# A transformer kernel on one core: two blocks side by side at the start of the dense mixture, weight conversions moved out of attention, another beginning

## The chip, the cores and the metric

One core of a Trainium2 chip. The metric is device time in microseconds of one execution of the whole program. Engines: TensorE (matmuls), VectorE (DVE), ScalarE (ACT), GpSimd (POOL), SyncE (SP, which issues most DMAs).

## What is computed

Three parts in a row, all in float32 with float64 inputs where the inputs came as such (the two weight matrices `w_in` and `w_out` of the first mixture arrive as float64 and are converted on the chip from their two 32-bit words).

```python
# 1. attention: batch 4, 8 heads, 512 local and 32 global positions, head size 64
s_g = scale * q_g @ concat(k_g, k_l).T;  out_g = softmax(s_g) @ concat(v_g, v_l)
s_ll = where(|i - j| <= 32, scale * q_l @ k_l.T, -1e9);  s_lg = scale * q_l @ k_g.T
out_l = softmax(concat(s_lg, s_ll)) @ concat(v_g, v_l)
x = concat(out_g, out_l) as 2176 tokens of 512
# 2. first mixture (dense): w_in 512 x 2048, w_out 2048 x 512
h = x @ w_in
g = where(h >= 1, h, where(h <= -1, 0, (h + 1) ** 2 / 4))
y = g @ w_out
# 3. second mixture: 8 experts, one chosen for each token
logits = (y / |y|) @ (emb / |emb|).T / tau;  e = argmax;  gate = softmax(logits)[e]
out = gate * (relu(y @ w1[e]) @ w2[e])
```

## The kernel before, in words

**Attention** runs in eight units (`Unit`, L310): unit n is batch n // 2 and four of the eight heads. A unit has four quarters k = 0 to 3. A quarter is: `scores` (L427: 16 small matmuls, then on VectorE a mask with a running minimum, on ACT an exponential), `fin` (L475: reciprocals on VectorE, normalising on GpSimd), `trans` (L491: transposes on TensorE, copies on ACT), `pval` (L512: the product with the values, copied to SBUF by ACT) and, after every second one, `gsum` (L538: a sum on VectorE and the store of the result to DRAM). Once per unit come `glob_s`, `glob_n` and `glob_t` (L383 to L425): the global queries' scores, their normalising on GpSimd, their transposes. Keys and queries of a unit are loaded by `ld_qk`, put in pair order by `pair` (a copy, on ACT for k and on VectorE for q, but on VectorE for unit 0), transposed and spread by `tr_k` and `tr_q`. `glob_load` and `glob_tr` (L161, L167) load and transpose the global keys and queries of all four batches, once.

**The order** is one list: `events` (L553) gives each step a mark, 16 marks to a unit and four to a quarter, and each engine's queue, SP's too, gets its instructions in the order of the marks. The offsets are in the table `AT` (L22): quarter k of unit n has its scores at 16 n + 4 k, its transposes 9.34 later, its value product 13.59 later. Each engine works strictly in its own order.

**Conversions.** `conv_load` (L232) loads a raw tile of 512 KB (128 rows of 512 float64); `conv_half` (L248) converts half of one: three bit operations on VectorE (L214, L217, L220); for a half of `w_in` then a rounded copy `winh` on ACT (L257) and the rest `winl` on GpSimd (L258). There are 32 raw tiles, 64 halves. `seq` (L228) is their order: 12 tiles of `w_in`, 12 of `w_out`, 4 of `w_in`, 4 of `w_out`. The marks `CV` and counts `CN` (L28) put 40 halves in attention; the other 24 go into the slots of the mixture's block 0. Two buffers hold raw tiles; the load of tile n + 2 is issued when tile n is converted.

**First mixture.** 17 tiles of 128 tokens in six blocks of 3, 3, 2, 3, 3 and 3 tiles. A slot g is one block bi and one f of 16: `up1` (L709: 12 matmuls, x and w_in each split into a rounded part and a rest, into a PSUM buffer `hps`, of which there are two), `act1` (L723: ReLU, square, then on VectorE the minimum and maximum, and by `wout` L743 the split of one row block of w_out), `act1b` (L739: the rest on VectorE), and, two slots later (LAG), `down1` (L751: 9 matmuls into `yp`). The main loop (L1322) walks g, block after block. A block's x comes back from DRAM by `x_load` (L681) and is split by `x_split` (L691) during the block before. When a block is done `y_out` (L608) copies and stores its output tiles, and the router's work on them (`logits`, 8 dot products on VectorE a tile, `choose`, `route3`) is spread by `pieces` (L776) over the slots of the next block; 3, 2, 3, 3, 3 and 3 tiles after the six blocks. `embed_bc` (L622) loads eight broadcast rows of 256 KB for them. Two up projections, `up1(0)` and `up1(1)`, are issued at the end of attention (marks 185.66 and 202.01), after all of its steps.

**Second mixture.** The most frequent expert runs densely over all blocks, the other tokens in gathered quads. The change does not touch it.

Of the kernel before, what the change touches and what calls it, by code (L numbers as in the profile page):

```python
# [9 lines left out]
F32 = mybir.dt.float32  # L10
# [22 lines left out]
def kernel(  # L33
# [19 lines left out]
    P = 128  # L53
# [107 lines left out]
    def glob_load(src, tag, bufs):  # L161
        t = mx.tile([P, H, D], F32, name="gl", tag=tag, bufs=bufs)
        for b in range(B):
            nc.sync.dma_start(out=t[b * G : (b + 1) * G], in_=src[b].rearrange("h s d -> s h d"))
        return t

    def glob_tr(src, isq):  # L167
        pt = ps.tile([P, NP, P], F32, name="pgl", tag="T")
        for hp in range(NP):
            nc.tensor.transpose(pt[:, hp, :], src[:, 2 * hp : 2 * hp + 2, :].rearrange("p h d -> p (h d)"), ident)  # L170
        if isq:
            nc.vector.tensor_copy(out=qgz[0:D, :, 0, :], in_=pt[0:D])
            nc.vector.tensor_copy(out=qgz[D:P, :, 1, :], in_=pt[D:P])
        else:
            nc.vector.tensor_copy(out=kgT, in_=pt)
# [49 lines left out]
    nin, nout = KD * DFF // CL, KF * DM // CL  # L225
    craw = {}

    seq = [*range(3 * KD), *range(nin, nin + 12), *range(3 * KD, nin), *range(nin + 12, nin + nout)]  # L228
    NCV = len(seq)
    ncv = sum(CN) // 2  # L230

    def conv_load(n):  # L232
        if n >= NCV:
            return
        i = seq[n]
        if i < nin:
            f, k = divmod(i, KD)
            src = win_u[:, k, 2 * f * CL : 2 * (f + 1) * CL]
        else:
            src = wout_u[:, i - nin, :]  # L240
        if n < ncv + 2:
# [4 lines left out]
        nc.sync.dma_start(out=raw.rearrange("p n t -> p (n t)"), in_=src)  # L246

    def conv_half(n, h):  # L248
        c0 = h * CC
        i = seq[n]  # L250
        raw = craw[n][:, c0 : c0 + CC, :]
        if i < nin:
            f, k = divmod(i, KD)
            wf = mx.tile([P, DM], F32, name="wf", tag="wf")[:, :CC]
            conv(raw, wf)
            hi = winh[2 * f + h][:, k, :]
            nc.scalar.copy(out=hi, in_=wf)  # L257
            nc.gpsimd.tensor_tensor(out=winl[2 * f + h][:, k, :], in0=wf, in1=hi.bitcast(F32), op=ALU.subtract)  # L258
        else:
            conv(raw, wof[(i - nin) // 2][:, (i - nin) % 2, c0 : c0 + CC])  # L260
# [1166 lines left out]
```

## Time and profile before

| | us |
|---|---|
| median of 3 runs (794.5 to 796.12) | 794.64 |
| the profiled execution's own time | 794.92 |
| its span, first to last instruction | 793.1 |
| TensorE busy | 759.5 |
| VectorE busy | 504.2 |
| ScalarE busy | 404.2 |
| GpSimd busy | 145.6 |

The profiled execution is one run; its span leaves out what lies before the first and after the last instruction. Busy times are sums over the span. A busy TensorE is not one at its peak: its instructions are pipelined and their ends are modelled. The program's stages follow each other: attention to about 166 us, the first mixture to about 558, then the second. The chain of waits is followed back from the last instruction: at each step to what released it.

### The profile page before, as it was taken

The page shows a single profiled execution, that of the slowest core. Times are in us where ns is not written, and L with a number is a line of the kernel's source. Part 1 is how long each engine was busy: PE and PEld are TensorE (multiplying, and loading weights), DVE is VectorE, ACT ScalarE, POOL GpSimd, SP SyncE. Part 2 cuts the span into 40 slices and gives each one's busy share as a digit, 9 for nine tenths or more (in the row PEclk, how much of TensorE's full clock was granted, in tenths as well). Part 3 has the DMA queues.
Part 4 walks back from the last instruction along what each step waited for, and adds up shares of the span by engine and source line. Part 5 has one row for each costly group of instructions (what it writes and reads, how often), then busy time and mean ns, then how long its engine had stood idle before and what let it go on. Part 6 is the DMA issues. An engine that isn't in the chain of part 4 may idle for free.

```text
span 793.1 us, 14812 instructions
## 1 busy us (share of the span) xinstructions
PE 759.5 (96%) x5115; PEld 640.8 (81%) x5115; DVE 504.2 (64%) x1513; ACT 404.2 (51%) x1011; POOL 145.6 (18%) x301
## 2 busy tenths in 40 slices
PE   6989986999999999999999999999999999999997
PEld 4767765789899898999889988989888777778775
DVE  3889986969876678867676677888786211221111
ACT  2989986845655556764655565665311121112100
POOL 4778885612100000000000001000002101010001
PEclk7899998989999999999999999999999999999999
DMA  7777877653252002001002001223207389454321
GB/s 184 202 211 225 221 195 216 189 160 121 81 160 66 2 1 80 1 28 40 0 1 67 1 1 67 93 79 90 73 0 265 100 308 309 136 179 120 107 93 37
DMA packets 73072, 89.40 MB, mean 113 GB/s; under 512 B 27440, under 2 KB 47920, under 8 KB 72992
## 3 DMA queue, kind: packets, MB, share of 16 engines
q1 hardware_dynamic: 71312, 83.42, 34.9%
q0 software_dynamic: 1680, 4.98, 1.6%
q8 instruction: 42, 0.69, 0.4%
q14 instruction: 38, 0.31, 0.1%
HBM read 79.77 MB, written 13.65 MB: 118 GB/s over the span
## 4 chain that ended last, share of the span: by engine, by line
PE 56%; issue 20%; DVE 11%; DMA 6%; ACT 4%; POOL 3%; SPq 1%; POOLq 0%; ACTq 0%; DVEq 0%
PE hps L718 22%; PE yp L761 22%; DMA out<-ob,ide 4%; PE eh L1186 2%; PE eo L1208 2%; DVE wf L217 1%; DVE sm L451 1%; ACT sm L461 1%; PE pv L524 1%; DVE wf L220 1%; POOL out L1220 1%; PE s L439 1%; PE ta L501 1%; PE pv L535 1%; DMA raw<-in_moe_w_out 1%
## 5 line engine op out<-in xcount | busy, mean ns | idle before, releaser
L718 PE MATMUL hps<-xh,winh 128*128 128x384 f32 (+1 forms) x384 | 126.3, 329 | 0.0
L718 PE MATMUL hps<-xl,winh 128*128 128x384 f32 (+1 forms) x384 | 126.1, 328 | 0.0
L718 PE MATMUL hps<-xh,winl 128*128 128x384 f32 (+1 forms) x384 | 125.7, 327 | 0.0
L761 PE MATMUL yp<-wol,gh 128*128 128x512 f32 x272 | 107.5, 395 | 0.0
L761 PE MATMUL yp<-woh,gh 128*128 128x512 f32 x272 | 107.3, 395 | 0.0
L1192 DVE SCALAR_TENSOR_TENSOR el<-eh,eg 128x384 fp32r<-128x384 f32 (+1 forms) x48 | 25.7, 535 | 118.4 <-ACT eg L1191 110.4
L1191 ACT ACTIVATE eg<-eh 128x384 fp32r<-128x384 f32 (+1 forms) x48 | 22.7, 474 | 120.5 <-PE eh L1186 108.7
L718 PEld LDWEIGHTS hps<-xh,winh 128*128 128x128 f32 x384 | 72.6, 189 | 4.0
L718 PEld LDWEIGHTS hps<-xh,winl 128*128 128x128 f32 x384 | 72.5, 189 | 3.8
L718 PEld LDWEIGHTS hps<-xl,winh 128*128 128x128 f32 x384 | 72.4, 189 | 0.0
L748 DVE TENSOR_TENSOR wol<-wof,woh 128x512 fp32r<-128x512 f32 x96 | 66.4, 692 | 1.3
L1186 PE MATMUL eh<-exh,wh 128*128 128x384 f32 (+1 forms) x192 | 65.3, 340 | 0.0
L1186 PE MATMUL eh<-exl,wh 128*128 128x384 f32 (+1 forms) x192 | 62.8, 327 | 0.0
L1186 PE MATMUL eh<-exh,wl 128*128 128x384 f32 (+1 forms) x192 | 62.7, 326 | 0.0
L1220 POOL DMA_INDIRECT out<-ob,ide x17 | 17.3, 1019 | 230.1 <-DVE ob L1217 227.0
L747 ACT CAST woh<-wof 128x512 fp32r<-128x512 f32 x96 | 58.0, 605 | 0.1
L461 ACT ACTIVATE sm<-sm,st 128x160 f32<-128x160 f32 x128 | 53.4, 426 | 8.5 <-DVE st L451 8.5
L761 PEld LDWEIGHTS yp<-wol,gh 128*128 128x128 f32 x272 | 51.1, 188 | 8.0
L761 PEld LDWEIGHTS yp<-woh,gh 128*128 128x128 f32 x272 | 51.1, 188 | 7.9
L483 POOL TENSOR_SCALAR pn<-sm,st 128x128 f32<-128x128 f32 x128 | 53.7, 438 | 19.0 <-DVE st L479 11.2
L1208 PE MATMUL eo<-wl,eg 128*128 128x512 f32 x136 | 53.8, 395 | 0.1
L1208 PE MATMUL eo<-wh,el 128*128 128x512 f32 x136 | 53.6, 394 | 0.0
(904 smaller groups left out, 1664.0 us busy)
## 6 DMA issues: line engine op xcount, KB each, us to landing
rw<-in_moe_w SPq DMA_DIRECT2D x128, 256.0 KB
raw<-in_moe_w_in SPq DMA_DIRECT2D x16, 512.0 KB
raw<-in_moe_w_out SPq DMA_DIRECT2D x16, 512.0 KB
k<-in_k_l SPq DMA_DIRECT2D x16, 256.0 KB
q<-in_q_l SPq DMA_DIRECT2D x16, 256.0 KB
xsc<-xs SPq DMA_DIRECT2D x16, 256.0 KB
ysc<-y SPq DMA_DIRECT2D x16, 256.0 KB
rw<-in_moe_w SPq DMA_DIRECT2D x8, 512.0 KB
```

The costliest lines, as they stand in the source:

```text
L217: nc.vector.scalar_tensor_tensor(out=du, in0=hi, scalar=0xC0000000, in1=du, op0=ALU.bitwise_and, op1=ALU.bitwise_or)
L461: nc.scalar.activation(out=sm[:, i, :], in_=sm[:, i, :], func=AF.Exp, scale=-1.0, bias=st[:, 0, i : i + 1], accum_out=st[:, 1, i : i + 1],)
L483: eng_of[AT["f4"][i]].tensor_scalar(out=pn[:, i, :].rearrange("p (c x) -> p c x", c=2), in0=sel(sm[:, i, :]), scalar1=st[:, 2, i : i + 1], ...
L718: nc.tensor.matmul(hp_[:, :n], lhsT=wt[:, kk, fs], rhs=xt, start=kk == 0 and i == 0, stop=kk == KD - 1 and i == 2)
L747: nc.scalar.copy(out=woh, in_=wof[f // 2][:, f % 2, :])
L748: nc.vector.tensor_tensor(out=wol, in0=wof[f // 2][:, f % 2, :], in1=woh.bitcast(F32), op=ALU.subtract)
L761: nc.tensor.matmul(B_.yp[i], lhsT=gt[:, cs], rhs=wt, start=f == 0 and k == 0, stop=f == KF - 1 and k == 2)
L1186: nc.tensor.matmul(hps[:, :n], lhsT=w[:, fs], rhs=x, start=kk == 0 and i == 0, stop=kk == KD - 1 and i == 2)
L1191: nc.scalar.activation(out=gh, in_=hps[:, :n], func=AF.Relu)
L1192: nc.vector.scalar_tensor_tensor(out=gl, in0=hps[:, :n], scalar=0.0, in1=gh.bitcast(F32), op0=ALU.max, op1=ALU.subtract)
L1208: nc.tensor.matmul(B_.yp[i], lhsT=a[:, cs], rhs=w, start=f == 0 and k == 0, stop=f == KF2 - 1 and k == 2)
L1220: nc.gpsimd.indirect_dma_start(out=outs[t], out_offset=bass.IndirectOffsetOnAxis(ap=ide[:, t : t + 1], axis=0), in_=ob, in_offset=None, bo ...
```

## The change

Five things. (1) Blocks 0 and 1 of the first mixture alternate, f by f (`items`), so that one split of `w_out` serves both (`wout`); block 1's sums take the PSUM buffers of tag T; x of both blocks is loaded and split in attention, x of block 2 at the end of the pair. (2) 18 halves are converted in attention, at other marks (`CV`, `cmarks`), and 46 in the pair's slots, in order of need: for each eighth m of the inner dimension two tiles of `w_in` and two of `w_out`. A tile of `w_in` now holds two row blocks of 256 columns. (3) The beginning: the first q load is issued on ACT's queue, only batch 0 of the global keys and queries is loaded and transposed before unit 0's global scores, the rest in units 0 and 1; the second quarter's scores of unit 0 move from mark 4 to mark 1; raw loads start later; 26 more small matmuls (`warm`). (4) The copies of k to pair order go to VectorE; the two early up projections move from behind all steps of attention to marks 134.5 and 136.5, ahead of the last value product (137.59). (5) `pieces` is computed by a rule and takes 0, 3, 4, 4, 3 and 3 tiles after the six blocks; output tiles 3, 4, 5 and 10 get other buffers (`YOB`).

```diff
-    ld_v=13.82, k0=10.74, q0=11.3, k1=15.74, q1=14.98, xl=116.97, xs=129.29, u0=185.66, u1=202.01, rk0=6.13,
-    rq0=8.31, rk1=11.03, rq1=11.75, e_k='A', e_q='V', e_g='P', bp=1, ev=10, le='PVPVV', e_kc='A', e_kd='A',
+    ld_v=13.82, k0=10.74, q0=11.3, k1=15.74, q1=14.98, xl=70.0, xs=84.9, xl1=118.5, xs1=130.1, u0=134.5, u1=136.5, rk0=6.13,
+    rq0=8.31, rk1=11.03, rq1=11.75, e_k='V', e_q='V', e_g='P', bp=1, ev=10, le='PVPVV', e_kc='A', e_kd='A',
...
-CV = [8.84, 10.77, 11.32, 11.44, 13.36, 16.6, 17.6, 23.12]
-CN = [4, 6, 4, 4, 4, 6, 6, 6]
+CV = [1.2, 5.2, 8.8, 12.84]
...
-    seq = [*range(3 * KD), *range(nin, nin + 12), *range(3 * KD, nin), *range(nin + 12, nin + nout)]
-    NCV = len(seq)
-    ncv = sum(CN) // 2
+    NCV = 4 * NC
+    ms = [16 * u + v for u in range(2 * B) for v in CV]
+    cmarks = [ms[2 + i * 28 // 17] for i in range(18)]
+    ncv = len(cmarks) // 2
...
+        m, r = divmod(n, 4)
...
+        if r < 2:
+            nc.sync.dma_start(
+                out=raw.rearrange("p (k n) t -> p k (n t)", k=2),
+                in_=win_u[:, 2 * r : 2 * r + 2, 2 * m * CC : 2 * (m + 1) * CC],
+            )
...
-                at(t0 + 4 * k, scores, n, k)
+                at(t0 + 4 * k if n or k != 1 else 1, scores, n, k)
...
-        at(1.92, glob_tr, qgl, True)
-        for u, c in enumerate(CN):
-            for j in range(c):
-                at(4 + 16 * u + CV[j * 8 // c], conv_half, *cvq.pop(0))
+        at(0.5, warm, 8)
+        at(1.5, glob_tr, qgl, True, 0, G)
+        at(1.6, warm, 8)
+        at(1.895, warm, 4)
+        at(2.0, conv_load, 0)
+        at(8.0, glob_load, k_g, kgl, [1, 2, 3])
+        at(8.0, glob_load, q_g, qgl, [1, 2, 3])
+        at(9.0, conv_load, 1)
+        at(22.5, glob_tr, kgl, False, G, P)
+        at(22.6, glob_tr, qgl, True, G, P)
+        for m in cmarks:
+            at(m, conv_half, *cvq.pop(0))
...
-        at(AT["xl"], x_load, 0)
-        at(AT["xs"], x_split, 0)
+        for bi, sfx in ((0, ""), (1, "1")):
+            at(AT["xl" + sfx], x_load, bi)
+            for i in range(2):
+                at(AT["xs" + sfx] + 2 * i, x_split, bi, [i])
...
+    items = [(bi, f) for f in range(KF) for bi in range(2)] + [(bi, f) for bi in range(2, NB) for f in range(KF)]
...
+    YOB = {3: 1, 4: 2, 5: 3, 10: 1}
...
     def wout(g):
-        f = g % KF
+        bi, f = items[g]
+        if bi == 1:
+            wq[g] = wq[g - 1]
+            return
...
-            B_.yp = [ps.tile([P, DM], F32, name=f"yp{i}", tag="y", bufs=3) for i in range(nt)]
+            B_.yp = [ps.tile([P, DM], F32, name=f"yp{i}", tag="T" if bi == 1 else "y", bufs=3) for i in range(nt)]
...
-            n = 2 if bi == 1 else 3
+            n = (0, 3, 4, 4, 3, 3)[bi]
...
+        work = []
+        for i, y in ty:
+            work += [(1.0, lambda i=i, y=y, e=e: logits(i, y, e, e + 1)) for e in range(E)]
+            work += [(0.0, lambda i=i, y=y: ysq(i, y)), (0.0, None)]
+            work += [(1.2, lambda i=i: choose(i, 1)), (0.0, None), (0.8, lambda i=i: route3(i, 1))]
+        lim = sum(c for c, _ in work) / 14.6
...
-        ld_qk(0, 0, lambda: gls.append(glob_load(k_g, "wf", 2)))
+        kgl, qgl = (mx.tile([P, H, D], F32, name="gl", tag="xl") for _ in range(2))
+        ld_qk(0, 0, nc.scalar)
+        glob_load(k_g, kgl, [0])
         ld_qk(0, 1)
-        qgl = glob_load(q_g, "wf", 2)
-        for i in range(2):
-            conv_load(i)
+        glob_load(q_g, qgl, [0])
         ld_v(0)
...
+                if g == 2 * KF - 2:
+                    x_load(2)
+                if g == 2 * KF - 1:
+                    x_split(2)
                 act1(g, hp_)
-                if bi == 0 and f > 0:
-                    conv_next(1 + (f <= 4 or f % 2) if NCV - ncv > 7 else 1)
-                    if f == KF - 2:
-                        conv_next(len(cvq))
-                        embed_bc()
+                if g == 0:
+                    conv_load(ncv)
+                    conv_load(ncv + 1)
+                if bi < 2 and g > 1:
+                    conv_next(1 if g % 4 == 1 else 2)
+                if g == 2 * KF - 3:
+                    assert not cvq
+                    embed_bc()
...
-                if f in (9, 11) and bi + 1 < NB:
+                if f in (9, 11) and 1 < bi < NB - 1:
                     x_split(bi + 1, [(f - 9) // 2])
...
-                if f == 4 and bi + 1 < NB:
+                if f == 4 and 1 < bi < NB - 1:
                     x_load(bi + 1)
```

## Rows read from the trace of the kernel before

In rows of stretches the busy times stand in the order TensorE, its weight loads, VectorE, ScalarE, GpSimd; then the granted clock, the busy share of the core's 16 DMA engines and GB/s.

**Rows 1.** Stretches, one per unit: span in us, length, then as above.

```profile
9.42:28.63 19.21, 15.99 (x144) 11.67 (x144) 11.91 (x58) 11.97 (x47) 7.29 (x19) 0.64 0.75 194
28.63:44.88 16.25, 15.07 (x211) 11.63 (x210) 15.49 (x64) 15.71 (x60) 13.80 (x31) 1.00 0.78 211
44.88:66.11 21.23, 18.02 (x210) 13.47 (x210) 17.52 (x74) 17.93 (x66) 15.42 (x34) 0.92 0.74 203
66.11:81.95 15.84, 14.98 (x210) 11.62 (x209) 15.09 (x63) 15.22 (x59) 13.77 (x31) 1.00 0.81 234
81.95:98.43 16.48, 15.04 (x210) 11.63 (x209) 15.42 (x65) 15.86 (x61) 13.91 (x31) 1.00 0.82 226
98.43:115.72 17.29, 15.36 (x210) 11.71 (x209) 15.04 (x65) 15.46 (x59) 13.89 (x31) 1.00 0.74 207
115.72:141.10 25.38, 18.62 (x210) 13.89 (x210) 18.78 (x80) 17.79 (x66) 13.56 (x32) 0.87 0.71 191
141.10:166.00 24.90, 21.81 (x271) 16.87 (x271) 21.60 (x82) 16.22 (x59) 14.60 (x32) 0.89 0.65 188
```

**Rows 2.** The chain that ended last, in the mixture: start, length, what.

```profile
248.43 2.10 PE hps L718 x12
250.53 2.08 PE yp L761 x9
```

**Rows 3.** Instructions in order of time, TensorE, unit 3: start, length, what, idle before.

```profile
66.11 0.77 PE L439 MATMUL s<-kw,qT 64*64 64x160 f32 x16
...
70.03 0.77 PE L439 MATMUL s<-kw,qT 64*64 64x160 f32 x16
...
72.84 0.82 PE L439 MATMUL s<-kw,qT 64*64 64x160 f32 x16
74.51 0.66 PE L420 MATMUL pgt<-ident,pg 128*128 128x128 f32 x4 [0.84 <-POOL pg L412]
...
78.32 0.77 PE L439 MATMUL s<-kw,qT 64*64 64x160 f32 x16
```

**Rows 4.** The chain that ended last, in units 2 and 6: loads in it.

```profile
50.09 5.58 DMA raw<-in_moe_w_in
...
122.74 6.84 DMA raw<-in_moe_w_out
```

**Rows 5.** Stretches, the conversions on VectorE alone (three instructions each): length, busy, count, clock, DMA.

```profile
9.42:166.00 156.58, 56.18 (x120) 0.91 0.74 204
166.00:232.00 66.00, 27.70 (x72) 0.99 0.37 118
```

**Rows 6.** Groups by line and shape, the whole span: count, busy us, mean ns, idle before.

```profile
L257 ACT CAST winh<-wf 128x256 fp32r<-128x256 f32 x32 | 13.1, 411 | 13.9 <-DVE wf L220 13.5
...
L329 ACT COPY kp<-k 128x512 f32<-128x512 f32 x14 | 8.9, 637 | 0.1
...
L638 DVE SCALAR_TENSOR_TENSOR jk<-y,ebchTh 128x512 bf16<-128x512 f32 x34 | 22.7, 685 | 0.0
```

**Rows 7.** Instructions in order of time, the beginning, VectorE and TensorE.

```profile
7.60 0.43 DVE L329 COPY qp<-q 128x512 f32<-128x512 f32 x1 [2.83 <-DMA q<-in_q_l]
...
15.47 2.67 PE L392 MATMUL sg<-kw,qgz 128*32 128x512 f32 x8 [0.84 <-DVE qgz L172]
```

**Rows 8.** Instructions in order of time, ScalarE, the end of attention.

```profile
156.57 1.57 ACT L702 CAST xh<-xl 128x768 fp32r<-128x768 f32 x2
...
168.98 0.58 ACT L732 ACTIVATE t__2994<-hps,half 128x384 f32<-128x384 f32 x1 [2.07 <-DMA xsc<-xs]
```

**Rows 9.** Stretches in the mixture: block 2; from a raw load's issue to its end.

```profile
299.05:344.50 45.45, 45.45 (x302) 41.27 (x300) 39.00 (x108) 30.36 (x68) 0.00 (x0) 1.00 0.11 36
...
199.63:202.85 3.22, 3.22 (x19) 3.00 (x18) 2.10 (x5) 2.04 (x5) 1.48 (x2) 1.00 0.51 163
```

**Rows 10.** Instructions in order of time, TensorE, a stall in block 0.

```profile
213.06 0.50 PE L761 MATMUL yp<-woh,gl__3372 128*128 128x512 f32 x1 [1.77 <-DVE gl__3372 L741]
```

More of the change, by code (lines that the diff above doesn't have):

```diff
@@ L159, with glob_load, glob_tr @@
     nc.gpsimd.memset(qgz, 0.0)
-    def glob_load(src, tag, bufs):
-        t = mx.tile([P, H, D], F32, name="gl", tag=tag, bufs=bufs)
-        for b in range(B):
+    def glob_load(src, t, bs):
+        for b in bs:
             nc.sync.dma_start(out=t[b * G : (b + 1) * G], in_=src[b].rearrange("h s d -> s h d"))
-        return t
-    def glob_tr(src, isq):
+    def glob_tr(src, isq, r0, r1):
         pt = ps.tile([P, NP, P], F32, name="pgl", tag="T")
         for hp in range(NP):
-            nc.tensor.transpose(pt[:, hp, :], src[:, 2 * hp : 2 * hp + 2, :].rearrange("p h d -> p (h d)"), ident)
+            nc.tensor.transpose(
+                pt[:, hp, :r1], src[:r1, 2 * hp : 2 * hp + 2, :].rearrange("p h d -> p (h d)"), ident[:r1, :r1]
+            )
         if isq:
-            nc.vector.tensor_copy(out=qgz[0:D, :, 0, :], in_=pt[0:D])
-            nc.vector.tensor_copy(out=qgz[D:P, :, 1, :], in_=pt[D:P])
+            nc.vector.tensor_copy(out=qgz[0:D, :, 0, r0:r1], in_=pt[0:D, :, r0:r1])
+            nc.vector.tensor_copy(out=qgz[D:P, :, 1, r0:r1], in_=pt[D:P, :, r0:r1])
         else:
-            nc.vector.tensor_copy(out=kgT, in_=pt)
+            nc.vector.tensor_copy(out=kgT[:, :, r0:r1], in_=pt[:, :, r0:r1])
     def y_rows(i):
@@ L274, in ld_qk @@
             h0 = NH * u.g + 2 * hl
-            nc.sync.dma_start(
+            (nc.sync if dst is u.k2 else qe).dma_start(
                 out=dst[:, 2 * hl : 2 * hl + 2], in_=src[u.b, h0 : h0 + 2].rearrange("h (p t) d -> p h t d", p=P)
             )
-            if between and dst is u.k2:
-                between()
     def ld_v(n):
@@ new lines, in pieces @@
+        for i, y in ty:
[3 more added lines that the diff above has]
+        lim = sum(c for c, _ in work) / 14.6
+        heads = [list(work[13 * j : 13 * j + 13]) for j in range(len(ty))]
+        slots = []
+        wait = [0] * len(ty)
+        while any(heads):
+            now, cost = [], 0.0
+            for j, h in enumerate(heads):
+                if not h or wait[j] > len(slots):
+                    continue
+                while h and cost + h[0][0] <= lim + 0.5:
+                    c, f = h.pop(0)
+                    if f is None:
+                        wait[j] = len(slots) + 1
+                        break
+                    now.append(f)
+                    cost += c
+                if h and wait[j] <= len(slots):
+                    break
+            slots.append(lambda now=now: [f() for f in now])
@@ L809, in pieces_end @@
+        return slots
     def pieces_end(*ty):
@@ L1284, with warm @@
     with tc.manual_schedule():
-        gls = []
-        ld_qk(0, 0, lambda: gls.append(glob_load(k_g, "wf", 2)))
+        kgl, qgl = (mx.tile([P, H, D], F32, name="gl", tag="xl") for _ in range(2))
+        ld_qk(0, 0, nc.scalar)
+        glob_load(k_g, kgl, [0])
         ld_qk(0, 1)
-        qgl = glob_load(q_g, "wf", 2)
-        for i in range(2):
-            conv_load(i)
+        glob_load(q_g, qgl, [0])
         ld_v(0)
-        wt = ps.tile([P, P], F32, name="wt", tag="T")
-        for _ in range(32):
-            nc.tensor.matmul(wt, lhsT=ones_bf, rhs=ones_bf, start=True, stop=True)
+        def warm(n):
+            wt = ps.tile([P, P], F32, name="wt", tag="T")
+            for _ in range(n):
+                nc.tensor.matmul(wt, lhsT=ones_bf, rhs=ones_bf, start=True, stop=True)
+        warm(32)
         pair(0, 0, "k")
@@ L1297 @@
         tr_k(0, 0)
-        glob_tr(gls[0], False)
+        glob_tr(kgl, False, 0, G)
         kw_g(0, 0)
         tr_q(0, 0)
+        warm(6)
         early = []
@@ L1353 @@
             if g < nsl:
-                if f == 4 and bi + 1 < NB:
+                if f == 4 and 1 < bi < NB - 1:
                     x_load(bi + 1)
-            if bi == NB - 2 and f == 15:
+            if bi == NB - 2 and f == KF - 1:
                 pick()
```

72 lines of the change are left out of this document (20 added, 52 removed).

## The prediction, made before the changed kernel was run

> **What bounds the kernel now.** I read the stretches first, cut where the first score matmuls of each attention unit start on TensorE [rows 1]. The eight units end at 166.0 us. After that TensorE is never idle for long in the first mixture: a slot there is one up projection of 2.10 us and one down projection of 2.08 us back to back, 4.18 us [rows 2]. So time can only come off before 166 us, or from the few holes behind it.
>
> Inside attention the units differ: 16.25, 15.84, 16.48 and 17.29 us for units 1, 3, 4 and 5 (mean 16.47), but 21.23 for unit 2 and 25.38 for unit 6 [rows 1]. In the four even ones ACT is busy for 15.2 to 15.9 us and DVE for 15.0 to 15.5: the two are full. TensorE is too, nearly. Its own row of work in unit 3 [rows 3]: from the scores of one quarter to the next 3.92, 2.81 and 5.48 us, then 3.63 to the start of unit 4 at 81.95 [rows 1]; 0.84 of the 5.48 is idle, behind GpSimd's normalised global row. Without that idle the four make 15.0 us. That is the floor of a unit.
>
> The two long units come from weights. The chain of waits shows two loads of raw weight, of 5.58 us at 50.09 and 6.84 us at 122.74 [rows 4]: VectorE, in order, stands at a conversion whose load is late, and masks, reciprocals and copies queue up behind it. The clock granted in those units is 0.92 and 0.87, a mean of the two levels 2.4 and 1.2 GHz, since TensorE had been idle and came back at the lower one [rows 1].
>
> **The change part by part, and its sum.** The sum is made against the profiled execution, 794.92 us (span 793.1 and 1.8 around it); the median of the runs is 0.28 lower.
>
> *Conversions out of attention.* Of 64 conversions of half a raw tile, 40 run in attention now and 18 after; 46 instead of 24 run in the mixture. 40 cost DVE 56.18 us, 1.40 each; in the mixture 24 cost 27.70, 1.15 each [rows 5]. So DVE loses 22 x 1.40 = 30.9 us in attention and gains 22 x 1.15 = 25.4 in the mixture. Of the 24 halves of w_in 10 stay: ACT loses 14 x 0.41 = 5.8 us [rows 6], GpSimd the 14 subtractions. The copies of k to pair order go from ACT to DVE: ACT loses 8.9 us [rows 6], DVE gains 14 x 0.43 = 6.0, by the same copy of q [rows 7]. The split of block 1 comes into attention: 1.57 us of ACT [rows 8], about as much of DVE. Over the eight units ACT goes from 126.2 to 113.1 us and DVE from 130.9 to about 107.8, so 14.1 and 13.5 per unit, below TensorE's 15.0. SP issues 11 raw loads of half a megabyte less in attention and one block load more, and each load that stays is issued most of a unit ahead of its conversion. So the two late loads should go. TensorE becomes the limit. Bounds for a unit: 15.0 (the floor) and 16.47 (the mean of the four that have no late load). I take 15.4, the floor and half the idle of 0.84, because the wait on GpSimd is a chain over four engines that only shortens where DVE ran a conversion ahead of it. Units 1 to 6 take 112.5 us now [rows 1], 6 x 15.4 = 92.4 after: **-20.1** (between -22.5 and -13.7).
>
> *The beginning.* The first q load goes to ACT's queue; only batch 0 of the global keys and queries is loaded and transposed at first; the raw loads move behind v; the second quarter's scores come right behind the first's; 26 small matmuls fill waits. DVE waited 2.83 us for q, until 7.60 [rows 7]; with no issues ahead of it most of that goes, 1.9. The global scores began at 15.47, behind the copy of the global queries, and their 8 matmuls took 2.67 us at a granted clock of 0.64 for the unit [rows 1, 7]; at the higher level that is 1.3 less. Together **-3.2**. Bounds: 0 (the same loads, the same engines), and -5.7, where scores start at 7.5 and unit 0 is as long as a later one (22.9 in place of 28.6).
>
> q is issued behind k and four loads of global keys, and DVE has idled for it from 4.77 to 7.60 [rows 7]. The Trainium skill (DMA: Bandwidth & Descriptors, Rules for kernel authors) says that spreading transfers over issuing engines gives no bandwidth, only issue time. By it q and k share the engines, about 1 us of my 1.9 is given back, and the sum would end 1 us higher.
>
> The other global loads, 6 small DMAs on SP, and their 8 transposes move into units 0 and 1; they add TensorE about 1 us there, hidden in unit 0's waits, or in unit 1 at worst 1 us more.
>
> *The end of attention.* The first two up projections now stand ahead of the last value product in TensorE's order. They look free, but I cost them at almost nothing. The first activation of the mixture waits for the store of the last attention tile, 2.07 us, until 168.98 [rows 8]: its tile lies where that one lay. Today the two up projections (4.2 us) run just then and hide the chain store, ReLU, square, combine, behind which the third up projection gets its PSUM buffer. Moved ahead, they delay the last value product by up to 4.2 us and leave the same hole open behind it. What is gained is the idle time ahead of that product: **-1.0**. Bounds: -4.2 if the tile waits for something earlier, +2.
>
> *The mixture.* Blocks 0 and 1 alternate in 32 slots, 133.8 us. DVE has 46 x 1.15 = 53 us of conversions in them and, at the rate of the later slots with their 18 dot products taken out (39.00 - 18 x 0.69 = 26.6 for 16 slots of two tiles [rows 6, 9]), about 60 more for three tiles with the output weights split once for both blocks: 113 of 134, where today single slots are full. The stall of 1.77 us at 213.06, where DVE's remainder came late [rows 10], should go: -1.8. Given back: no logits run in the pair, so the two-tile block 2 gets three tiles of them in place of two. Its 45.45 us hold 39.00 of DVE; 8 dot products at 0.69 and 1 us of choosing make 45.5 [rows 6, 9]: full. I take +1.0, bounds 0 and +3.
>
> A wait is added: block 2's load is issued after the last up projection of block 0, behind 2 MB of broadcasts on SP, and its split stands on ACT ahead of the last activation of block 1. TensorE has three products, 6.3 us, until it needs the split. A half megabyte landed within 3.22 us of its issue here [rows 9], the split adds about 2.5: 5.7. So 0, at worst +1.5, and the last activation has two slots until its down projection. Output tiles 3, 4, 5 and 10 change buffers at no cost; the routing of 4 tiles in blocks 3 and 4 has a DVE that the 4.18 us slots leave room on. **-0.8.**
>
> Sum: -3.2 - 20.1 - 1.0 - 0.8 = -25.1, so 769.8 for a profiled execution and **769.5 us** for the median.
>
> **The rivals.**
>
> *Only the late loads go.* ACT and DVE have less to do, but each unit's length is set by the order of waits, and stays at 16.47. For it: TensorE's idle of 0.84 stands behind a chain that passes four engines [rows 3]. Against: unit 3, with its lighter load, already reaches 15.84 [rows 1]. Units 1 to 6 then give -13.7: 776.
>
> *Everything falls into place.* Units at 15.0, a start of -5.7, an end of -4.2, no loss in block 2: -22.5 - 5.7 - 4.2 - 1.8 = -34.2: 760.5. Against it the end of attention, where the wait on the store stays as long as the tiles lie where they lie [rows 8].
>
> *Slower: the raw loads of the mixture are late.* 23 loads go through two buffers, each issued when the one two before is converted; seven halves in four slots leave a load 4.8 us. A load of 3.22 us [rows 9] fits. One of 6.84, as with attention's DMA load [rows 4], would hold DVE 2 us each time. DVE's room is 21 us, so what is over 21 comes out on TensorE, and the 25 us won are gone when 23 x (load - 4.8) is over 46: from 6.8 us per load. At 7.5 it is 23 x 2.7 - 21 = 41 lost, 811 us. The DMA share in the mixture is 0.37 against attention's 0.74 [rows 5], and the new loads of w_in are in pieces of half the length; so unlikely. *That the change does nothing* would need the two late loads to stay late and ACT's relief to be off the path; I leave 0.01 for it.
>
> **How the numbers follow.** Forecast 0.56, only the late loads 0.25, everything 0.14, slower 0.04, nothing 0.01. The first three are faster by far more than 0.2% (1.6 us, about what runs of this kernel can tell): 0.95, same 0.01, slower 0.04. The forecast's own range, with its bounds combined, is 764 to 776. The range has to take in the other two: 760.5 with its doubt about the floor, and 776 with a start that gains nothing (+3.2) and the losses of the mixture (+3): 759 to 782.
>
> **What would show it.** Units 1 to 6 of 15 to 15.8 us, none over 17, TensorE's idle in them behind GpSimd alone and ACT below 95%; no raw load in the chain of waits; scores at 7.5 us and the second quarter's within 3 us of them; about 4 us of idle TensorE between the last value product and the third up projection; no DVE wait for a raw load in the mixture; DVE over 95% in block 2, with stalls of TensorE of 1 us in all. The prediction is wrong if units stay above 16 us, if DVE waits for raw loads in the mixture, or if the mixture from its third up projection to block 3 takes over 3 us more than now.

## The result, and the profile of the changed kernel

The changed kernel takes 801.76 us (median of 7 runs, 798.57 to 808.72), the kernel before 794.64 beside it. The ratio is 1.0101, 95% interval 1.0062 to 1.0139: slower by 7 us, where I forecast 25 faster. The profiled execution took 808.72 us (span 806.8), the slowest of the seven.

Cut at four places that both traces have (first scores of unit 1 and of unit 7, first and last activation of the dense mixture), the two spans, 793.1 and 806.8 us, compare so. The last column is a repaired kernel that is explained below, run 8.

| from, to | before | after | difference | forecast | run 8 |
|---|---|---|---|---|---|
| start to unit 1 | 28.63 | 29.82 | +1.2 | -3.2 | 29.94 |
| units 1 to 6 | 112.47 | 118.09 | +5.6 | -20.1 | 98.53 |
| unit 7 to first activation | 27.88 | 24.45 | -3.4 | -1.0 | 24.43 |
| first to last activation | 377.57 | 384.38 | +6.8 | -0.8 | 378.11 |
| last activation to end | 246.55 | 250.06 | +3.5 | 0 | 247.09 |

The differences add up to 13.7 us, where the medians differ by 7.1: this was the slowest execution. Traces of the same attention differ: units 1 to 6 take 118.09 us here and 110.96 in run 3 below, which changes only the mixture; in the kernel before they take 112.47, and 109.68 in run 6, which adds work only behind them. So the gain of 20.1 us is in neither trace of the new attention, and the loss of 5.6 in one of them alone.

The stretches of the changed kernel, units 0 to 7, the last one up to the end of attention (columns as in [rows 1]):

```profile
9.66:29.82 20.16, 15.42 (x164) 11.89 (x164) 12.52 (x61) 11.24 (x45) 8.32 (x20) 1.00 0.60 153
29.82:54.79 24.97, 19.33 (x217) 14.99 (x217) 14.94 (x68) 16.05 (x62) 12.16 (x31) 0.79 0.66 164
54.79:70.52 15.73, 15.07 (x210) 11.58 (x209) 13.36 (x61) 13.46 (x54) 10.79 (x27) 1.00 0.74 199
70.52:85.79 15.27, 14.81 (x211) 11.59 (x210) 12.59 (x63) 13.69 (x55) 10.27 (x26) 1.00 0.84 217
85.79:105.07 19.28, 16.59 (x211) 12.58 (x210) 13.17 (x64) 15.80 (x61) 13.17 (x33) 0.91 0.79 212
105.07:125.25 20.18, 16.78 (x210) 12.53 (x209) 14.90 (x66) 15.92 (x58) 11.04 (x29) 0.92 0.51 133
125.25:147.91 22.66, 17.76 (x211) 13.70 (x210) 12.70 (x61) 14.27 (x55) 11.86 (x32) 0.85 0.79 198
147.91:172.00 24.09, 22.93 (x296) 18.73 (x295) 12.77 (x58) 16.89 (x61) 11.50 (x31) 1.00 0.25 73
```

Units 2 and 3 are what I forecast for all six, 15.73 and 15.27 us. VectorE's and ScalarE's work did come down: unit 3's 12.59 and 13.69 us stand against 15.09 and 15.22 in [rows 1]. But units 1, 4, 5 and 6 are 19 to 25 us long, with no engine full. Something makes them wait, and after it the granted clock is a mean of 1.2 and 2.4 GHz again (0.79 to 0.92).

Whom they wait for is in SyncE's own queue. Its instructions in order of time (start, time it takes to issue, what):

```profile
21.86 0.38 SPq L243 DMA_DIRECT2D raw<-in_moe_w_in  x1
30.16 0.35 SPq L248 DMA_DIRECT2D raw<-in_moe_w_out  x1
30.55 0.43 SPq L292 DMA_DIRECT2D va<-in_v_l  x1
31.08 5.62 SPq L299 DMA_DIRECT2D vgz<-in_v_g  x4
...
39.61 0.61 SPq L277 DMA_DIRECT2D k<-in_k_l  x1
...
111.90 0.38 SPq L545 DMA_DIRECT2D xsc<-xs  x1
124.13 0.37 SPq L243 DMA_DIRECT2D raw<-in_moe_w_in  x1
...
133.33 0.55 SPq L277 DMA_DIRECT2D k<-in_k_l  x1
```

Read the gaps. After a raw load at 21.86 SyncE issues nothing for 8 us, after a store at 111.90 nothing for 12 us. Both times the next instruction is a raw load, and it waits for its buffer: `conv_load(n + 2)` stands in the order right behind the conversion of tile n, and VectorE, in its own order, has not done that yet. Its last instruction of those two conversions ends at 30.13 and 124.10 (start, length):

```profile
29.70 0.43 DVE L220 SCALAR_TENSOR_TENSOR wf<-raw,wf 128x256 uint32<-128x256 uint32 x1
...
123.68 0.42 DVE L220 SCALAR_TENSOR_TENSOR wof<-raw,wof 128x256 uint32<-128x256 uint32 x1
```

Everything behind it on SyncE waits too: the ten issues of the next unit's v, then k and q of the unit after. So k is issued at 39.61 and 133.33, and VectorE, which since the change copies k itself, stands for it:

```profile
43.93 0.43 DVE L329 COPY kp<-k 128x512 f32<-128x512 f32 x1 [5.08 <-DMA k<-in_k_l]
...
137.19 0.43 DVE L329 COPY kp<-k 128x512 f32<-128x512 f32 x1 [3.53 <-DMA k<-in_k_l]
```

In all VectorE waits 16.1 us for k, in five waits. The first copy of all has 5.3 of them (3.8 before, when only unit 0's k copies were on VectorE); the other 10.8 are new. The chain of waits passes the same place:

```profile
39.61 4.30 DMA k<-in_k_l
43.93 0.43 DVE kp L329
```

SyncE stood at raw loads before the change too, some 37 us in all in attention, up to 6.7 at a time (32 and 11.9 after it). But there those that waited stood behind the next unit's v, k and q, which were issued by then. Its queue in unit 1 of the kernel before, where the second of the two raw loads waits 4.2 us:

```profile
29.98 0.55 SPq L275 DMA_DIRECT2D k<-in_k_l  x1
...
33.53 4.95 SPq L246 DMA_DIRECT2D raw<-in_moe_w_in  x2
```

The second loss is in the mixture. VectorE's and TensorE's instructions in block 2 (start, length, what, idle before):

```profile
340.86 0.96 DVE L721 TENSOR_TENSOR xl<-xl,xh 128x768 fp32r<-128x768 f32 x1 [0.42 <-ACT xh L720]
...
342.39 0.17 DVE L669 TENSOR_TENSOR ohot<-iota,ixf 128x8 bf16<-128x8 f32 x1
```

```profile
339.05 0.28 PE L736 MATMUL hps<-xl,winh 128*128 128x256 f32 x1
342.61 0.17 PE L680 MATMUL rk<-ohot,tri_bf 128*128 128x8 bf16 x1 [3.28 <-DVE ohot L669]
...
342.72 0.77 PE L782 MATMUL yp<-woh,gh 128*128 128x512 f32 x1
...
345.42 0.41 PE L736 MATMUL hps<-xh,winh 128*128 128x256 f32 x1
```

TensorE stands 3.28 us, not for the mixture's own data but for the one-hot row of the router (`ohot`), which VectorE writes late. VectorE is busy for 3.73 of the 4.38 us before the hole, and a half split of the next block's x stands right before the choice of the expert, 0.96 us and 0.42 of waiting for ScalarE's part of it. Then TensorE's matmuls take 0.41 us where the same shape took 0.28 ahead of the hole: from 342.72 to 347.98 the granted clock is 0.50, the lower level, and it was 1.00 from 334.92 to the hole. From the first activation of block 2 to that of block 3 it is 54.54 us, before 47.67.

The third is 3.5 us at the program's end, in code that the change doesn't touch:

```profile
793.54 0.40 PE L1226 MATMUL eo<-wh,eg 128*128 128x512 f32 x1
796.04 0.59 PE L1226 MATMUL eo<-wl,eg 128*128 128x512 f32 x1 [2.11 <-issue]
796.43 0.63 PE L1226 MATMUL eo<-wh,el 128*128 128x512 f32 x1
```

TensorE waits 2.11 us for nothing that the profile shows, then runs at the lower clock (0.50 from 796.04 to 799; 0.63 us a matmul in place of 0.40). The trace of before has no such row.

The beginning, VectorE, to be read with [rows 7], and the end of attention, ScalarE, with [rows 8]:

```profile
5.27 0.88 DVE L329 COPY kp<-k 128x512 f32<-128x512 f32 x1 [5.27 <-DMA k<-in_k_l]
6.07 0.42 DVE L329 COPY qp<-q 128x512 f32<-128x512 f32 x1
```

```profile
166.92 0.45 ACT L329 COPY xs<-pv 128x320 f32<-128x320 f32 x1
172.03 0.43 ACT L329 COPY xs<-pv 128x320 f32<-128x320 f32 x1 [4.66 <-PE pv L535]
172.35 0.59 ACT L750 ACTIVATE t__2910<-hps,half 128x384 f32<-128x384 f32 x1
```

### The profile page after: what moved, and what is told of

Its sections match the earlier page's. It is cut to its first block, busy times and chain, and to the rows that moved or that the text cites. A ratio compares the mean times of both kernels' runs of the same rounds, so it can differ in the third digit from the quotient of the medians.

```text
span 806.8 us, 14839 instructions
## 1 busy us (share of the span) xinstructions
PE 765.2 (95%) x5149; PEld 646.9 (80%) x5149; DVE 496.1 (61%) x1514; ACT 390.7 (48%) x981; POOL 138.2 (17%) x301
## 4 chain that ended last, share of the span: by engine, by line
PE 62%; issue 20%; DMA 5%; DVE 5%; ACT 4%; POOL 3%; SPq 1%; POOLq 0%; ACTq 0%; DVEq 0%
PE hps L736 23%; PE yp L782 23%; DMA out<-ob,ide 4%; PE eh L1204 2%; PE s L439 2%; PE eo L1226 2%; PE pv L524 2%; PE ta L501 2%; PE pv L535 2%; ACT sm L461 2%; PE pq L379 1%; POOL out L1238 1%; DMA k<-in_k_l 1%; DMA raw<-in_moe_w_in 1%; PE sg L392 1%
## 5 line engine op out<-in xcount | busy, mean ns | idle before, releaser
L483 POOL TENSOR_SCALAR pn<-sm,st 128x128 f32<-128x128 f32 x128 | 50.8, 415 | 34.1 <-DVE st L479 13.3
L769 DVE TENSOR_TENSOR wol<-wof,woh 128x512 fp32r<-128x512 f32 x80 | 55.3, 692 | 1.1
L1226 PE MATMUL eo<-wh,eg 128*128 128x512 f32 x136 | 53.8, 395 | 0.0
```

Of the source, the lines that this page charges most:

```text
L483: eng_of[AT["f4"][i]].tensor_scalar(out=pn[:, i, :].rearrange("p (c x) -> p c x", c=2), in0=sel(sm[:, i, :]), scalar1=st[:, 2, i : i + 1], ...
L769: nc.vector.tensor_tensor(out=wol, in0=wof[f // 2][:, f % 2, :], in1=woh.bitcast(F32), op=ALU.subtract)
L1226: nc.tensor.matmul(B_.yp[i], lhsT=a[:, cs], rhs=w, start=f == 0 and k == 0, stop=f == KF2 - 1 and k == 2)
```

## The experiments

Theories. **A**: the order on SyncE. **B**: the engine of the k copies. **C**: the conversions themselves are too much for VectorE. **D**: the router's work beside block 2. **E**: TensorE's program has grown past a block of code. All runs in one table: the ratio to the kernel before with its interval, then the five stretches of the table above in each run's own trace. A trace is one execution: runs 8, 10, 11 and 12 have the same beginning, and reach unit 1 at 28.82 to 31.18 us, so 2 us in that column show nothing by themselves.

| run | ratio | to unit 1 | units 1-6 | to 1st act. | mixture | rest |
|---|---|---|---|---|---|---|
| the change | 1.0101 [1.0062, 1.0139] | 29.82 | 118.09 | 24.45 | 384.38 | 250.06 |
| 1 k copies on ACT | 1.0069 [1.0048, 1.0090] | 27.58 | 111.92 | 24.45 | 384.17 | 248.97 |
| 2 raw loads behind | 0.9985 [0.9963, 1.0006] | 29.76 | 104.59 | 24.43 | 383.26 | 249.07 |
| 3 two tiles in block 2 | 1.0057 [1.0027, 1.0086] | 28.30 | 110.96 | 24.43 | 376.60 | 249.01 |
| 4 run 2, first two loads first | 0.9976 [0.9949, 1.0002] | 27.67 | 101.45 | 24.44 | 384.18 | 249.56 |
| 5 runs 1, 3 and 4 together | 0.9890 [0.9858, 0.9923] | 26.41 | 102.84 | 24.43 | 378.14 | 251.99 |
| 6 before, 34 matmuls more | 1.0066 [1.0043, 1.0088] | 29.61 | 109.68 | 27.23 | 377.57 | 252.22 |
| 7 run 5, 34 matmuls less | 0.9863 [0.9832, 0.9894] | 28.82 | 102.49 | 24.41 | 378.15 | 246.33 |
| 8 run 5, old beginning | 0.9844 [0.9818, 0.9870] | 29.94 | 98.53 | 24.43 | 378.11 | 247.09 |
| 9 run 8, k copies on DVE | 0.9873 [0.9853, 0.9894] | 32.65 | 100.14 | 24.44 | 378.12 | 246.54 |
| 10 run 8, raw loads ahead | 0.9996 [0.9976, 1.0016] | 30.22 | 114.71 | 24.44 | 378.10 | 246.64 |
| 11 run 8, split later | 0.9831 [0.9813, 0.9849] | 28.82 | 95.37 | 29.40 | 378.10 | 246.31 |
| 12 run 8, three tiles | 0.9920 [0.9894, 0.9947] | 31.18 | 98.04 | 24.44 | 381.54 | 246.61 |

### Run 1: the k copies back on ScalarE

```diff
-    ... e_k='V', ...
+    ... e_k='A', ...
```

> The k copies go back from VectorE to ScalarE, all else as in the changed kernel (801.76 us). Theory A (order on SyncE: the raw loads stand ahead of the next unit's v, k and q loads and wait there for VectorE) expects k to land as late as now, near 44 us for unit 2, and the transposes to wait for it all the same: VectorE alone gets free, 796 to 802. Theory B (VectorE takes the waits for k in its own order, 16.1 us in 5 waits, and that is the loss) expects most of these back: about 787, and units 1, 4, 5 and 6 near 16 us each in place of 25.0, 19.3, 20.2 and 22.7.

Measured 0.3% less than the change, with overlapping intervals; units 1, 5 and 6 are still 22.9, 20.8 and 21.0 us. B falls as the main cause: behind the first copy VectorE no longer waits for k, but ScalarE does, and VectorE waits for q instead, which stands behind k in SyncE's queue (and 2.44 us again at 130.67):

```profile
39.91 0.62 ACT L329 COPY kp<-k 128x512 f32<-128x512 f32 x1 [2.16 <-DMA k<-in_k_l]
...
42.52 0.43 DVE L329 COPY qp<-q 128x512 f32<-128x512 f32 x1 [2.30 <-DMA q<-in_q_l]
```

### Run 2: the raw loads behind the next unit's loads

```diff
-            if n < ncv - 2 or n >= ncv:
+            if n >= ncv:
                 conv_load(n + 2)
...
+        slots_ = [16 * u + v for u in range(8) for v in (6.5, 15.3)]
...
+            if i % 2 and i // 2 < ncv - 2:
+                at(min(v for v in slots_ if v > m), conv_load, i // 2 + 2)
```

> The raw loads of the third to ninth converted piece are issued behind the next unit's v, k and q loads (or behind a store of xs at 6.5 of a unit), not at the mark of the conversion that frees their buffer. Theory A expects SyncE's idle times of 8.3 us (21.86 to 30.16) and 12.2 us (111.90 to 124.13) gone, k for unit 2 to be issued near 31 in place of 39.61, and about 13 of the 16.1 us of VectorE's waits for k with it: 786 to 790. Theory B expects the copies to wait as before, since the loads themselves wait for the copy that frees the k buffer: 798 or more. Theory C (the conversions themselves are too much work for VectorE in a unit) expects no more than 2 us either way.

1.2% less than the change (9 us). In the trace units 1 to 6 are 13.5 us shorter than in the change's, 6.4 shorter than in run 3's, and VectorE's waits for k fall from 16.1 us to 5.5, of which the first copy has 4.7. Units 1 and 6 come down to 19.1 and 16.3 us; unit 5 stays at 21.6, for a reason that run 11 shows. The conversions are all still there, so C falls, and the median, 792.08, lies 2 us above A's range.

### Run 3: two tiles beside block 2

```diff
-            n = (0, 3, 4, 4, 3, 3)[bi]
+            n = (0, 2, 5, 4, 3, 3)[bi]
```

Two tiles are spread over the slots by the list of the kernel before, five over 15 slots.

> The block of two tiles has the router work of two tiles beside it, as before the change, in place of three; the block behind it has five in place of four. Theory D (in block 2 VectorE has 2.9 us of work for 2.82 us of TensorE a slot, so that a half split of x pushes it behind, TensorE stands 3.28 us at 339.3 for the choice of an expert and then runs at half clock for some 5 us) expects 5 to 6 us back: 796. The rival (the same work is only moved, and block 3 stalls in its place) expects 800 to 803.

The mixture takes 376.60 us, 7.8 less; TensorE does not stall in block 2, nor in block 3. The runs give 3.5 us (1.0057 against 1.0101), less than the one trace, and the intervals overlap; run 12 tests D again, where they do not.

### Run 4: and the first two raw loads at the very beginning

```diff
-        at(2.0, conv_load, 0)
...
-        at(9.0, conv_load, 1)
...
+        conv_load(0)
+        conv_load(1)
         def warm(n):
```

> As the kernel with the raw loads behind, and the first two raw loads are also issued at the very beginning, behind the v loads of unit 0, in place of marks 2.0 and 9.0. Theory A expects the wait of 6.78 us for the first raw piece (issued at 17.4, landed at 24.2) to go too, so that unit 0 and 1 follow each other by about 19 and 16 us: 780 to 785. Theory C expects no gain over the kernel with the raw loads behind. A rival on the beginning (the raw loads take the bandwidth that v and k need) expects the first scores of units 0 and 1 later and a loss of 1 to 4 us against that kernel.

Attention ends 5 us earlier in the trace than in run 2 (first activation at 153.56 against 158.77), but unit 1 is still 18.98 us and the ratios overlap: 791.71 in place of A's 780 to 785. The 6.78 us were the load's time from issue to landing; VectorE stood for it only 1.08 us.

### Run 5: the edits together

> The changed kernel with four things mended together: raw loads behind the next unit's loads, the first two at the very beginning, k copies on ScalarE, and two tiles beside block 2. If the three losses are separate, the gains add: 10 us (load order) + 4 to 8 us (block 2) + 0 to 2.5 us (copies) off 801.8: 782 to 788, 7 to 12 us below the kernel before. If they hide one another (what attention gains, the mixture's start gives back), it comes out no lower than the kernel with both raw-load edits, 791.

0.9890, 785.24 us: inside the range of separate losses and below 791, so the gains add. Its rest of 251.99 us is the longest yet, by the stall near the end and the lower clock behind it.

### Runs 6 and 7: 34 matmuls more, 34 less

Run 6 edits the kernel before, run 7 the kernel of run 5:

```diff
+        at(AT["u0"] - 0.1, warm34)
```

```diff
-        at(0.5, warm, 8)
...
-        at(1.6, warm, 8)
-        at(1.895, warm, 4)
...
-        warm(32)
+        warm(24)
...
-        warm(6)
```

> The kernel before with 34 more small matmuls on TensorE, put ahead of the first up projection, where TensorE stands anyway; their product is not used. The changed kernel has 34 matmuls more than the kernel before (5149 against 5115), and in all five traces of its family TensorE stands 1.6 to 2.1 us for nothing the profile shows, about 28 matmuls before its end, with an 8 KB instruction packet landing just before it goes on, then runs some 2.7 us at half clock; the trace of before has neither. Theory E (the end of TensorE's program has grown into one more block of code that is fetched late) expects the same stall here and 3 to 3.5 us more than before. The rival (the stall comes from the changed order of the mixture) expects no stall and the time of before within 1 us.

> The kernel with all four edits, and 34 of the small matmuls that keep TensorE busy in the beginning left out (26 between the steps of the beginning, 8 of the first 32; their product is not used), so that TensorE has 5115 matmuls, as before the change. Theory E expects no stall near the end and 3 to 3.5 us less than with them. The rival expects the stall to stay and the beginning to run at half clock for longer, 0 to 2 us more.

Run 6 is slower than before by 0.66% (5 us), and its trace shows the stall in a kernel that has nothing else of the change:

```profile
785.31 0.39 PE L1209 MATMUL eo<-wl,eg 128*128 128x512 f32 x1 [1.93 <-issue]
...
786.32 0.63 PE L1209 MATMUL eo<-wh,el 128*128 128x512 f32 x1
```

Its stretch from the last activation to the end is 252.22 us, before 246.55: 5.7 more. Run 7 has no such row, and 246.33. All seven traces with 5149 matmuls have such a stall, of 1.6 to 2.3 us, all seven with 5115 have none: it comes with the number of TensorE's instructions, not with the order of the mixture. Two things that I had expected of it are not so: 17 or 18 matmuls follow it, not 28, and the lower clock (0.63 us a matmul) follows only in three of the seven, the change and runs 5 and 6; in runs 1 to 4 the matmuls behind it take 0.39 to 0.40. The end is 2.4 to 3.0 us longer than before in these four, 3.5 to 5.7 in those three. In all seven that stall a 16 KB packet of instructions lands 1.3 to 1.7 us before TensorE goes on; the 8 KB packet that I had named is not there in runs 1, 5 and 6. That the 16 KB packet is TensorE's own next block is argued from this, not shown: such packets land near the end of traces without a stall as well (783.49 in that of before). The Trainium skill (Runtime: NRT & Kernel Launch, Instruction fetch mechanics) says that an engine fetches its code in 16 KiB blocks while it runs the one before, and that crossing a boundary is mostly hidden. If the stall is such a crossing, 1.6 to 2.3 us of it are not hidden here.

The interval of run 7 overlaps that of run 5 (0.9863 against 0.9890, 2.1 us): that the end is 5.7 us shorter is in the trace alone. Its beginning, with fewer small matmuls, is 2.4 us longer there, no more than equal beginnings differ.

### Run 8: the beginning of the kernel before

Run 5 with all of the beginning undone: global rows loaded and transposed whole, second scores at mark 4, q on SyncE, no small matmuls between; the two raw loads go ahead of v again.

> The kernel with all four edits and the beginning of the kernel before: global rows loaded and transposed whole, the second scores of unit 0 at mark 4, q on SyncE's queue, no small matmuls between; it has 5115 matmuls too. My forecast gave the new beginning 3.2 us, so this should be 3 us above the kernel with 34 matmuls fewer. The rival (k itself lands late in the new beginning, and the second transposition of the global rows is put on VectorE in unit 1) expects it to be equal or up to 4 us lower, with unit 1 near 16 us in place of 19.

0.9844: it beats both kernels, the one before by 12 us, and is no slower than run 7, which has the new beginning: the rival was right, and my 3.2 us were not there. In units 1 to 6 it wins 4.0 us against run 7, of which 2.4 in unit 1, which has no second transposition of global rows now. That holds in all traces with the loads in this order: unit 1 takes 16.3 to 16.9 us in runs 8, 9, 11 and 12, and 19.0 to 19.6 with the new beginning (runs 2, 4, 5 and 7). Units 1, 5 and 6:

```profile
29.94:46.80 16.86, 15.28 (x209) 11.71 (x209) 12.38 (x61) 15.94 (x62) 12.54 (x31) 1.00 0.59 165
...
93.88:112.21 18.33, 15.08 (x211) 11.58 (x210) 14.35 (x63) 16.19 (x60) 11.19 (x28) 1.00 0.69 184
112.21:128.47 16.26, 14.86 (x211) 11.59 (x210) 12.48 (x62) 15.30 (x59) 10.25 (x28) 1.00 0.80 212
```

The clock is 1.00 in all three, and k for unit 2 is issued 10 us earlier than in the changed kernel, ahead of the raw load:

```profile
29.82 0.55 SPq L277 DMA_DIRECT2D k<-in_k_l  x1
...
32.03 0.41 SPq L248 DMA_DIRECT2D raw<-in_moe_w_out  x1
```

### Run 9: run 8 with the k copies on VectorE

> The kernel with the four edits and the old beginning (0.984 of the kernel before), with the k copies on VectorE again, as in the change. Theory A (the engine of the copies costs only where k is late) expects no more than 1 us either way, and waits of VectorE for k under 3 us in all. Theory B (the copies on VectorE are a loss of their own) expects 2 to 4 us more.

0.9873 against 0.9844, 2.3 us, with intervals that overlap; VectorE waits 6.5 us for k, 2.8 of it beyond the first copy. Theory A's two numbers are missed, and B's 2 to 4 us are just reached. So a small loss by the engine of the copies can't be excluded. It is not the main one: run 10 has that with the copies on ScalarE.

### Run 10: run 8 with the raw loads ahead again

This undoes run 2's edit alone.

> The kernel with the four edits and the old beginning, with the raw loads of the third to ninth piece back at the mark of the conversion, ahead of the next unit's v, k and q loads on SyncE. Theory A expects the loss of 8 to 10 us to come back, most of it in units 1, 5 and 6, so 789 to 791. The rival (the late loads hurt only together with the new beginning, which issues more on SyncE in unit 0, and with the k copies on VectorE) expects less than 3 us.

0.9996 against 0.9844: 1.5%, 12 us back, more than expected, and where expected:

```profile
30.22:52.99 22.77, 18.19 (x209) 13.80 (x210) 12.68 (x63) 17.63 (x65) 13.59 (x36) 0.85 0.72 182
...
100.31:122.23 21.92, 16.81 (x210) 12.58 (x210) 14.80 (x66) 17.72 (x63) 10.74 (x30) 0.92 0.54 144
122.23:144.93 22.70, 17.97 (x211) 13.88 (x210) 11.90 (x59) 15.17 (x57) 11.00 (x31) 0.85 0.81 202
```

The same three units are 4 to 6 us longer, nothing else is: 16.2 us in units 1 to 6, within 1 us in all other stretches. Here the k copies are on ScalarE and the beginning is the old one, so neither is needed for the loss. The waits are for what stands behind the raw loads on SyncE. In units 1 and 6 VectorE waits for q; in unit 5 ScalarE waits for a store of `xs` that is issued behind v, and there the rows don't show which wait pushed it back:

```profile
43.90 0.43 DVE L331 COPY qp<-q 128x512 f32<-128x512 f32 x1 [3.33 <-DMA q<-in_q_l]
...
111.87 0.42 ACT L331 COPY xs<-pv 128x320 f32<-128x320 f32 x1 [2.30 <-DMA xsc<-xs]
...
135.61 0.43 DVE L331 COPY qp<-q 128x512 f32<-128x512 f32 x1 [3.66 <-DMA q<-in_q_l]
```

These waits add up to 9.3 us, the three units are 15.9 us longer than in run 8. TensorE came back from them at the lower clock: its busy time there grows by 7.8 us for the same matmuls, at a granted clock of 0.85 to 0.92 in place of 1.00. A stands.

### Run 11: the split of block 0 later

```diff
-    ... xl=70.0, xs=84.9, ...
+    ... xl=100.0, xs=117.0, ...
```

> The kernel with the four edits and the old beginning, with the load and the split of block 0's tokens moved from marks 70 and 84.9 (unit 5) to 100 and 117 (unit 7). Theory C' (unit 5 is 18.3 us in place of 16 because VectorE, already with a conversion and the copies of a unit in it, takes 2.4 us of the split) expects unit 5 at 16 us and the first up projection 2 us earlier: 779. The rival (the split then delays VectorE in unit 7, behind which the mixture starts) expects no change, 781, with the gap from unit 7 to the first up projection 2 us longer than its 24.4.

Unit 5 comes down from 18.33 to 15.08 us, and the stretch from unit 7 to the first activation grows from 24.43 to 29.40. ScalarE now does the splits of both blocks in unit 7, and VectorE waits for the last of them:

```profile
92.81:107.89 15.08, 14.62 (x210) 11.60 (x210) 13.05 (x61) 14.52 (x58) 10.87 (x28) 1.00 0.76 213
```

```profile
146.94 1.83 DVE L717 TENSOR_TENSOR xl<-xl,xh 128x768 fp32r<-128x768 f32 x2 [5.10 <-ACT xh L716]
```

In the trace both theories were right, the rival with 5 us in place of its 2; the time is the same as in run 8 by the intervals, and this one beats both kernels too. Load and split were moved together, so which of the two lengthened unit 5 is not separated.

### Run 12: run 8 with three tiles beside block 2 again

> The kernel with the four edits and the old beginning, with three tiles' router work beside block 2 again and four beside block 3, as in the change; it has 5115 matmuls, so no stall at its end clouds the reading. Theory D expects TensorE to stand some 3 us in block 2 and then run at half clock, the mixture (first to last activation) to take 384 us in place of 378, and 6 us more in all: 0.991 to 0.993 of the kernel before. The rival (with attention mended VectorE enters block 2 with less behind it, and the stall is gone) expects 0.984.

0.9920 against 0.9844, 6 us. The stall is the same as in the changed kernel:

```profile
323.71 0.17 PE L676 MATMUL rk<-ohot,tri_bf 128*128 128x8 bf16 x1 [3.27 <-DVE ohot L665]
...
323.81 0.48 PE L778 MATMUL yp<-woh,gh 128*128 128x512 f32 x1
```

But in this one execution, the fastest of its six, the clock stayed up behind it (next rows of that shape at 0.39 and 0.40), and the mixture is 3.4 us longer, not 6. In the four other traces with this hole (the change, runs 1, 2 and 4) the lower clock follows. D stands; its price is 3.4 us, and near 6 where the clock falls as well.

## Why the prediction was wrong

**The step that failed** is the largest, the conversions out of attention: "each load that stays is issued most of a unit ahead of its conversion. So the two late loads should go", with units at 15.4 us. The raw loads do come early enough: VectorE waits for one only once in attention, 1.1 us in unit 0, and not in units 2 and 6 any more (1.2 and 4.2 us before). But I looked at when a load is issued and not at what it holds up. `conv_load` waits on SyncE for VectorE to be done with a conversion, and at the new marks (12.84 of a unit, say) it stands just ahead of v (13.82), k (14.55) and q of the units after; at the old marks no load stood between 5.6 and 14.77 of a unit, so none just ahead of v. I listed SyncE's loads, fewer in number, and did not walk its queue past the one that waits. The term was +5.6 in place of -20.1, or -1.5 by run 3's trace. With that order mended too (run 8, from which run 10 differs by it alone) units 1 to 6 take 98.53 us, and with the split out of unit 5 95.37: -13.9 and -17.1, within my bounds of -13.7 to -22.5 (run 11 gives 5.0 of it back behind unit 7). The value of 15.4 a unit holds for units 2 and 3 of the changed kernel and of run 8 (15.1 to 15.9) and was too good by about 1 us for units 1, 4 and 6 of run 8. It was too good by 2.9 for unit 5, where the split of block 0 now lies: I had priced a split in attention as work, not as a wait of VectorE for ScalarE in front of the masks.

**The k copies.** I counted 6.0 us of VectorE's time and nothing else. The copy brings its wait for the load along, onto the engine that all the masks queue on: 10.8 us of new waits. Runs 1 and 9 put its own price near 2 us, not clearly above nothing.

**The beginning**, -3.2 forecast, +1.2 measured. The +1.2 is not clear of the spread: traces with this beginning reach unit 1 at 27.58 to 29.82 us (the change and runs 1 to 3), those of the kernel before and run 6 at 28.63 and 29.61. A gain of 3.2 is in none. q's copy is 1.5 us earlier than in [rows 7], but the first copy of k waits until 5.27 us, in the trace of before until 3.78; in all traces it starts at 4.7 to 5.3 us with the new beginning and at 3.7 to 3.9 with the old one. This is what the Trainium skill (DMA: Bandwidth & Descriptors, Rules for kernel authors) led me to price at 1 us: a second issuing engine brings no bandwidth. The rows agree, and the price was a little more. First scores came at 9.66, not 7.5. The global scores did run at the higher clock, 1.08 us in place of 2.67, but they began 1.9 us later than in [rows 7], and the chain of waits then goes through the first raw load, which starts later in the change and which I gave no price (an instruction, and a piece of the chain):

```profile
17.38 1.08 PE L392 MATMUL sg<-kw,qgz 128*32 128x512 f32 x8
```

```profile
17.42 6.78 DMA raw<-in_moe_w_in
```

What the beginning lost besides is in unit 1, where the rest of the global rows is transposed; I had 1 us at worst for it, and run 8 against run 7 shows 2.4 in that unit (16.86 against 19.25).

**The end of attention**, -1.0 forecast, -3.4 measured, by the mechanism described: ScalarE waits 4.66 us for the last value product, behind the two early up projections, and the third one starts late. The idle time ahead of that product was worth more than I took; the bound was -4.2.

**The mixture**, -0.8 forecast, +6.8 measured. The pair of blocks behaves as described: one wait of VectorE for a raw load, of 0.1 us, no stall of TensorE from 180 to 300 us, 130.69 us from first activation to the first of block 2 in place of 131.60. The term for block 2 was mis-sized: +1.0, bounds 0 and +3, measured 54.54 - 47.67 = +6.9. I found VectorE full there and took a full engine to cost its surplus. Two things were missing: the split of x ahead of the router's choice, which TensorE waits for in its own order, and the lower clock after the hole. Blocks 3 and 4, whose routing of 4 tiles I had at nothing, are 0.7 and 0.2 us longer.

**The end of the program**, nothing forecast, +3.5 measured. I gave the matmuls added at the beginning no price beyond their own time; run 6 shows that 34 more, put elsewhere and without the rest of the change, bring the stall.

**The rivals.** My slower case, raw loads late in the mixture, did not come: it had the right kind of mechanism (a load holds an in-order engine) in the wrong queue. "Only the late loads go" does not fit either, since units 1, 4, 5 and 6 got new waits. The chance of 0.04 for slower was far too small for a change that reorders a queue with waiting issues in it.

**What stays open.** The profiled execution of the change has 118.09 us in units 1 to 6, run 3 with the same attention 110.96. The waits in such a chain vary from one execution to the next; what tips it was not tried. Whose code the late instruction packet holds is not shown either.

## What to carry to other kernels

A DMA issue that waits for a buffer is a wait on the issuing engine: list what stands behind it in that queue, and put loads that must wait behind loads that need not (12 us here, for moving seven issues). When a copy moves to another engine, its wait for data moves too. And an engine that was full on average stalled another here not by its surplus but by the one late result that this one waited for in its order.

## What the runs showed of the hardware

34 small matmuls, put into idle time of TensorE at the end of attention, lengthened the program's end by 5.7 us (run 6: a stall of 1.93 us, and the lower clock after it, 0.63 us a matmul). All seven traces with 5149 matmuls have such a stall, of 1.6 to 2.3 us; in four of them the clock stays up behind it. And a hole of 3.27 to 3.28 us in TensorE's work is followed by the lower clock in four traces (0.41 us a matmul in the changed kernel) and not in a fifth (0.28 in run 12), so the same hole costs 3.4 or some 6 us.
